# One written-out order of 1169 steps replaced by another in a fused attention and mixing kernel

## The chip, the cores and the metric

The kernel runs on one core of a Trainium2 chip. The metric is device time in microseconds (us), the median of the runs shown. The engines are called as in the profile: PE (TensorE, matrix products) with PEld (its weight loads), DVE (VectorE), ACT (ScalarE), POOL (GpSimd) and SP (SyncE, which here issues the DMAs).

## The reference

```python
# q, k, v, f_logit: (4, 8, 768, 48)
f = 1 / (1 + exp(-f_logit))
for t in range(S):                                  # gated linear attention
    state = f[:, :, t, :, None] * state + einsum('bhd,bhe->bhde', k[:, :, t], v[:, :, t])
    y[:, :, t] = einsum('bhd,bhde->bhe', q[:, :, t], state)
x = y.transpose(0, 2, 1, 3).reshape(4, 768, 384)
theta = x @ w_theta                                 # mixing, w_theta (384, 384)
zr, zi = x * cos(theta), x * sin(theta)
u = x + einsum('ts,bsd->btd', w_tok_r, zr) + einsum('ts,bsd->btd', w_tok_i, zi)
return u + maximum(u @ w_ch, 0)
```

The weights come as 64-bit floats and are turned into 32-bit ones on the chip.

## The kernel before

The sequence of each of the four batches is cut into six chunks of 128 tokens, so that there are 24 chunks, m = 0 to 23. The tile framework runs with a manual schedule: the tuple ORDER names every step in turn, the n-th occurrence of a name being its n-th instance, and each engine gets its instructions in the order in which the steps stand there. Semaphore waits follow from the data and from the buffers. A suffix moves a step from its usual engine: /P to POOL, /D to DVE, /A to ACT. A suffix does nothing for a step whose function names its engine outright (d2 and ro). PLACES says which buffer of its kind each tile gets: "b" are the four single PSUM banks, "a" the two wide PSUM tiles, "z" the rotated values and the raw weights, "wp" the weights, "ut" the three buffers of the result.

The steps of a chunk in attention:

- lf, lk, lq, lv load the gate, key, query and value (SP).
- gc clamps the gate (DVE, or POOL, line 269), go opens it with an exponential and a logarithm (ACT, lines 274 and 275), gs is the running sum (DVE, line 279), ge takes two exponentials (ACT, lines 286 and 287), gp keeps the chunk's end (POOL), gq and gk multiply query and key (lines 294 and 299).
- ke transposes the key (PE, line 347), kt copies it out of PSUM, up builds the state sums (PE, line 362), sa and st add them up, sm fades the state. sc makes the scores (PE, line 333), ma masks them (DVE, line 339). qs and ou make the output (PE, lines 393 and 401), xc copies it, xt transposes it (PE, line 411), xs copies that into the result tile.

The steps of the mixing:

- lw loads a part of the weights; d1, d2, d3 decode it (DVE line 215, ACT line 220, DVE lines 225 and 226), di scales it, d4 and d5 split it in a high and a low half (lines 176 and 250; e4 and e5 do so for w_ch).
- th makes the angles (PE, line 442); for m from 6 on it takes the split forms that xh and xl make. tn, se, ab bring the angle into range, tr takes sine and cosine (ACT, lines 465 and 466) and ro multiplies them with x (DVE, line 475). zh and zl split the product.
- f0, f1, f2 are the token products, 48 of each (PE, line 498); for the first batch (n below 12) in full 32 bits, four profiled matmuls each, after that six matmuls in the faster form. v adds the sum to the result tile, uh and ul split it, c is a channel product (PE, line 516), cv finishes (DVE, line 530), so stores (SP, line 534).

tr and the pair go and ge need different ACT function tables, and each change from one to the other loads a table (lines 259 and 465). Line 176 is a helper that copies for many steps.

Of the kernel before, what the change touches and what calls it, by code (L numbers as in the profile page):

```python
# [17 lines left out]
B, H, S, D = 4, 8, 768, 48  # L18
DM = H * D
P = 128  # L20
# [32 lines left out]


PLACES = {
    "a": "0110110101001010110101010101010101010101010101010",
    "b": ("012301230120123023300300002121123222230230203120310202001031023333312312023011203100000023"
        "1030303030032123123211120303031"),
    "f": "012012012012012012012012",
    "k": "012012012012012012012012",  # L60
    "q": "012012012012012012012012",
# [3 lines left out]
    "ut": "01201201",  # L65
    "v": "012012012012012012012012",
    "w": "010101010101010101010101",
    "wp": "0123456789abcdefghijklmno013245687cd",
    "x": "012012012012012012012012",
    "z": "0123450123412342342350421350421350421",  # L70
}
ORDER = (
# [36 lines left out]
)  # L109


# [627 lines left out]
```

## Time and profile before

| | us |
|---|---|
| median of three runs | 337.82 |
| lowest and highest run | 337.38, 338.60 |
| time of the profiled execution | 338.16 |
| span of its instructions | 335.5 |

The profiled execution took 338.16 us, 2.66 us more than the span of its instructions. PE is busy for 316.8 us of the span; matmul ends are modelled, and short waits between matmuls can hide in that number.

### The profile page before, as it was taken

How to read it: one execution, taken by the hardware profiler on the slowest of the kernel's cores; microseconds unless marked ns; L12 is line 12 of the kernel's file. 1: busy time of each engine (PE TensorE's matmuls, PEld its weight loads, DVE VectorE, ACT ScalarE, POOL GpSimd, SP SyncE). 2: the span in 40 equal slices, each digit the busy share in tenths (PEclk: the TensorE clock that was granted, in tenths of full speed). 3: DMA queues.
4: the chain of work that ended last, by engine and by line, in shares of the span. 5: the costliest groups of instructions: out<-in, count | busy, mean ns of one | idle time of the engine just before them, and what ended most of it. 6: DMA issues, size and time to landing. Idle time of an engine off the chain costs nothing.

```text
span 335.5 us, 9996 instructions
## 1 busy us (share of the span) xinstructions
PE 316.8 (94%) x4320; PEld 280.7 (84%) x4320; DVE 243.4 (73%) x394; ACT 192.9 (58%) x321; POOL 112.3 (33%) x109
## 2 busy tenths in 40 slices
PE   0798999999999999999999999999999999999993
PEld 0685676567676789999999999999999999999992
DVE  5999999999999899968659777774526677441031
ACT  6789977787696799847468253953805342310010
POOL 2452074318100146265371248143800521103110
PEclk9999999999999999999999999999999999999998
DMA  7989779758660463240405353250122102000022
GB/s 266 395 244 304 254 249 340 249 181 308 243 212 17 150 225 111 91 156 15 130 3 168 115 160 117 88 178 0 33 73 79 49 2 73 0 2 0 0 73 77
DMA packets 21619, 45.54 MB, mean 136 GB/s; under 512 B 2369, under 2 KB 5441, under 8 KB 21569
## 3 DMA queue, kind: packets, MB, share of 16 engines
q1 hardware_dynamic: 21568, 44.84, 39.6%
q8 instruction: 36, 0.59, 0.7%
q14 instruction: 15, 0.11, 0.1%
HBM read 40.11 MB, written 4.72 MB: 134 GB/s over the span
## 4 chain that ended last, share of the span: by engine, by line
PE 83%; DVE 9%; ACT 2%; DMA 2%; issue 2%; DVEq 0%; ACTq 0%
PE pm L498 47%; PE pch L516 10%; PE pth L442 9%; PE wide L401 4%; PE wide L393 3%; PE wide L333 3%; PE pxt L411 2%; PE psk L347 2%; PE wide L362 2%; DVE f L279 2%; DMA out_dram<-ut 1%; DVE z L475 1%; DVE raw L215 1%; DMA f<-in_f_dram 1%; DVE k L299 1%
## 5 line engine op out<-in xcount | busy, mean ns | idle before, releaser
L498 PE MATMUL pm<-wp,z 128*128 128x384 f32 x648 | 117.1, 336 | 0.0
L498 PEld LDWEIGHTS pm<-wp,z 128*128 128x128 f32 x648 | 112.4, 188 | 0.0
L498 PE MATMUL pm<-value,z 128*128 128x384 f32 x144 | 49.3, 487 | 0.2 <-DVE z L475 0.2
L516 PE MATMUL pch<-uhl,wch 128*128 128x384 f32 x216 | 40.2, 339 | 0.4 <-DVE ut L176 0.4
L498 PEld LDWEIGHTS pm<-value,z 128*128 128x128 f32 x144 | 26.3, 190 | 15.9 <-DVE value L226 0.5
L516 PEld LDWEIGHTS pch<-uhl,wch 128*128 128x128 f32 x216 | 37.5, 188 | 1.0 <-DVE ut L176 0.7
L290 POOL COPY pes<-p 128x4 f32<-128x4 f32 x24 | 11.4, 476 | 72.6 <-ACT p L286 68.2
L502 DVE TENSOR_TENSOR ut<-pm,ut 128x384 f32<-128x384 f32 x24 | 13.1, 552 | 29.8 <-PE pm L498 29.8
L176 ACT CAST uhl<-ut 128x384 fp32r<-128x384 f32 x18 | 9.2, 509 | 41.5 <-DVE ut L502 41.5
L279 DVE TENSOR_TENSOR_SCAN f<-carry,f 128x512 f32<-128x512 f32 x24 | 29.1, 1222 | 0.7 <-ACT f L275 0.7
L433 POOL TENSOR_TENSOR xl<-ut,xh 128x384 fp32r<-128x384 f32 x13 | 13.5, 1041 | 46.1 <-DVE xh L176 29.1
L286 ACT ACTIVATE p<-f 128x512 f32<-128x512 f32 x24 | 15.1, 628 | 21.7 <-DVE f L279 21.3
L509 POOL TENSOR_TENSOR uhl<-ut,uhl 128x384 fp32r<-128x384 f32 x13 | 13.5, 1047 | 37.0 <-DVE uhl L176 18.6
L347 PE MATMUL psk<-ident,k 128*128 128x128 f32 (+1 forms) x96 | 16.8, 302 | 8.9 <-DVE k L299 8.8
L269 POOL TENSOR_SCALAR f<-f 128x512 f32<-128x512 f32 x14 | 23.3, 1668 | 1.5 <-DMA f<-in_f_dram 1.5
L530 DVE SCALAR_TENSOR_TENSOR ut<-pch,ut 128x384 f32<-128x384 f32 x24 | 13.0, 553 | 14.7 <-PE pch L516 14.4
L482 POOL TENSOR_TENSOR z<-w,z 128x768 fp32r<-128x768 f32 x9 | 17.4, 1931 | 17.8 <-ACT z L176 9.6
L442 PE MATMUL pth<-wth,xh 128*128 128x384 f32 x108 | 23.0, 348 | 0.0
L299 DVE SCALAR_TENSOR_TENSOR k<-f,k 128x512 f32<-128x512 f32 x24 | 19.5, 813 | 3.7 <-ACT f L287 3.6
L401 PEld LDWEIGHTS wide<-v,sc 64*64 64x64 f32 x768 | 15.0, 140 | 8.1 <-issue 4.7
L347 PEld LDWEIGHTS psk<-ident,k 128*128 128x128 f32 (+1 forms) x96 | 11.9, 148 | 11.6 <-POOL pes L290 8.8
L475 DVE TENSOR_TENSOR w<-w,x 128x768 f32<-128x768 f32 x18 | 18.1, 1010 | 4.0 <-ACT w L466 4.0
(84 smaller groups left out, 607.3 us busy)
## 6 DMA issues: line engine op xcount, KB each, us to landing
v<-in_v_dram SPq DMA_DIRECT2D x24, 384.0 KB, 4.4
f<-in_f_dram SPq DMA_DIRECT2D x24, 256.0 KB, 3.6
k<-in_k_dram SPq DMA_DIRECT2D x24, 256.0 KB, 4.1
q<-in_q_dram SPq DMA_DIRECT2D x24, 256.0 KB, 3.9
raw<-in_w_r_dram SPq DMA_DIRECT2D x12, 384.0 KB, 5.1
raw<-in_w_i_dram SPq DMA_DIRECT2D x12, 384.0 KB, 5.6
out_dram<-ut SPq DMA_DIRECT2D x21, 192.0 KB, 2.4
raw<-in_w_theta_dram SPq DMA_DIRECT2D x3, 384.0 KB, 5.5
```

What stands on the lines that cost most here:

```text
L269: on(nc.vector).tensor_scalar(ft, ft, F_MIN, None, op0=ALU.max)
L279: nc.vector.tensor_tensor_scan(fl, carry[:, pairs(h)].rearrange("p n t -> p (n t)"), fl, 0.0, ALU.mult, ALU.add)
L286: nc.scalar.activation(ps_[m][:, pairs(h)], ft, AF.Exp, scale=-1.0)
L299: nc.vector.scalar_tensor_tensor(kt, loaded["f", m][:, pairs(h)], E_TOP, kt, op0=ALU.min, op1=ALU.mult)
L347: nc.tensor.transpose(psks[m][:used(m), p, :], loaded["k", m][:, p, :used(m)], ident)
L401: nc.tensor.matmul(out[HALF[t], j, p, :], scs[m][HALF[a], j, p, :], v2[HALF[a], t, p, :], start=(t == 0 and m % NC == 0 and p == 0), stop= ...
L433: on(nc.vector).tensor_tensor(xls[m], src, xhs[m], op=ALU.subtract)
L442: nc.tensor.matmul(pths[m], l, r, start=(n == 0), stop=(n == len(ms) - 1))
L475: nc.vector.tensor_tensor(zs[m] if full else w, w, xs[m].unsqueeze(1).to_broadcast([P, 2, DM]), op=ALU.mult)
L482: on(nc.vector).tensor_tensor(zs[m][:, 0], ws[m], zs[m][:, 1], op=ALU.subtract)
L498: nc.tensor.matmul(pms[g, d], l, r, start=(s == 0 and i == 0), stop=(s == NC - 1 and i == len(ms) - 1))
L516: nc.tensor.matmul(pcs[g, d], l, r, start=(es[0] == 0 and n == 0), stop=(es[-1] == KD - 1 and n == len(ms) - 1))
```

## The change

The same 1169 steps stand in another order, and the tables of buffers follow it. No function changes, and each name occurs as often as before. The suffixes differ for some steps. DVE's steps by suffix: tn/D 8 for 6, xs/D 9 for 6, uh/D 12 for 6, xh/D as before, one di/D, d4/D 3 for 4, zh/D 6 for 9, kt/D and xc/D 4 for 5. POOL's: gq/P 11 for 9, xl/P 13 for 11, zl/P 13 for 9, sm/P 10 for 11, ul/P 10 for 13. ACT's: ab/A 17 for 14. The diff has all rows of the first third that the prediction speaks of, a stretch of the later part and the end.

```diff
--- before
+++ after
 PLACES = {
-    "a": "0110110101001010110101010101010101010101010101010",
-    "b": ("012301230120123023300300002121123222230230203120310202001031023333312312023011203100000023"
-        "1030303030032123123211120303031"),
+    "a": "0110110011001011001010101010110101010101010101010",
+    "b": ("012301230231202030020222223102131331001201230210212012022020313113103032031201301232321230"
+        "2320320202103213231213012210321"),
...
-    "wp": "0123456789abcdefghijklmno013245687cd",
-    "z": "0123450123412342342350421350421350421",
+    "wp": "0123456789abcdefghijklmno01245679deh",
+    "z": "0123450123412341341350412350412350412",
 }
 ORDER = (
-    "lf gc go lf gc go lf gs lk lq gc gs ge gk gq ke go gp lv sc ge gp gs lk lw lq kt lv lf gk d1 lk lw gq/P lf",
-    "up lq sa d2/P ke kt st ge d3 di d4 qs lv up ma gp ou xc lw sm/P sa gk ke st d1 lf d2 gq gc/P go sm/P d5 gs",
-    "qs gc/P d1 kt lk sc up go sa ma st ge gp gk lq lk d3 lv xt xs lf ou xc gq gs di d2/P gc/P ke kt lq xt go d3",
-    "gs th lw gc ge gp tn se lv gq qs gk sc up ma lq d1 xs go gs sm/P ab/A th ge gq ke kt lk gp ou sa st sm xc xt",
-    "gk d2 xs qs d3 sc up lw ge tr ma tn ro se lv ab gp lq ke kt th tn se sa st ou xc f1 xt xs/D lk qs gk sc tr",
-    "up ma sm/P lf lf d1 ab/A tr ro ro/P ke kt/D gc/P gc/P go sa lv th f0 go gs ou xc gq/P sc up lf gs ma qs sa",
-    "st ge lk gk xt gp f0 d4 f1 tn se xs th lq d2/P lw ke kt d3 sm lk gq/P ou xc/D tn ge se lv d1 sc up ma qs",
-    "d2/P xt f1 f2 f2 xs sa lw gc/P d1 ab ab/A d2 d3 d3 lw d1 f2 lw go gs d5/P th tr ro st tn sm/P gp lv lq gk d1",
-    "gq lq se tr d2 lk f0 ab/A f0 f1 ou ke ro f0 lf tr xc qs d3 kt sc up lw lw d1 xt ro/P f0 d2 d3 d2/P xs f1 f1",
-    "f1 d3 gc/P f1 d1 v lq ge d2 lv go lf xh gp gk gq/P sa st v ke ma xl/P ou sc kt up sm/P gs ge xc/D qs xt sa",
-    "st d4 gc/P xs d4/D f2 d4 ma lk gq lw d1 d2 lf gc/P th tn f2 f2 d3 lw d1 go lq gk ke d3 f1 go gs gs f1 uh kt",
...
-    "sc up xc ma gq qs ke kt/D sa f2 f2 ul uh ul/P f1 f0 ro/P v uh lv ul v c c xh/D cv cv lq c cv zh lf ou xc/D",
-    "sc up v ma gp ge sa qs xl/P uh/D uh gp ul ul gc/P go xt gq xt zl/P lk gk th tn se st ab tr lv sm/P c c so so",
-    "so lf xs/D cv gc/P lk c xh/D xl th zl/P xs xh xl/P ro/P ke kt ou xc/D cv sc up qs xt tn zh/D f0 lv se ab/A",
-    "cv xs th sa st f1 f1 zl/P f1 lq lq go ma so so xh tn/D se ab/A f2 f2 f2 so gs ge gp gs gk tr ro/P tr sm ke",
...
-    "se ab/A zh/D zl tr ro f2 f2 zh zl f0 so f1 f0 f1 f1 f1 f0 v uh/D f1 f2 f1 f1 f1 f2 v f2 so v uh/D uh ul/P f0",
-    "f2 f2 f0 f0 f0 f0 f0 v f2 ul/P ul/P c c cv cv so f1 c cv v so so uh uh f2 f2 v ul/P c ul/P uh ul c c rv cv",
-    "cv cv",
+    "lf gc go gs ge lf lf gc gc/P gp lk gk lq lq lk lk gq go gs go gs ge gp lv ke kt sc lf gq lq up gc gk ke sa",
+    "st ge gq/P qs go gp lv kt up gk sm/P ke gs ge lw d1 d2/P ma ou lw d1 xc lf lk sa st d2/P lv lf lq sc gc/P kt",
+    "qs lw d3 di lk d4 lv lq gk gc/P up ma sm/P go d3 di/D xt sa xs ou xc go lw gs ke gp gq st gs d1 ge gk gq lf",
+    "lf lv th sm qs sc kt up ma tn lq gp lw xt xs/D sa ke d2 st ou se th lk ge ab gp sm/P kt tr xc/D xt xs d3 ro",
+    "tn sc qs up gc/P gc/P th sa ma ou lk go go xc se gs f1 gk lv tn/D ke st gq/P gs ab/A xt xs/D d1 lq qs ge lv",
+    "kt sc up tr d2 se th ma sm/P sa ro/P gk ab/A gp tr d4/D d1 lk d4/D lq sc ou ke kt ro/P lw f0 xc xt xs d3 qs",
+    "up sa tn se d1 lv gq/P ge gq/P ma th st f0 qs tn/D lk d2/P ab/A tr gk se ou ke f2 f2 kt d5 xc d2/P d3 sm d3",
+    "ro/P lf lf lw xt lw d1 sc up lq xs th ma lw gc/P go gs f1 f1 f1 lv ou ab/A sa d2 lf gp d1 st d2/P gc/P d3 d3",
+    "lw go qs tn f2 f2 ge gk se gs tr ro d1 f0 gc/P xc ke ab/A gp sm tr ro kt/D f0 d2/P go f2 sc lv up xt xs d3",
+    "d5 f0 lk gq ge f2 f0 d4 f1 lw d1 d4 d4 gs lq gq/P d4 sa f1 v d2/P gk ke kt ma ou xc lq st uh/D xh/D lw v uh",
+    "v uh d1 xl/P d3 d2/P d1 sc up qs gp lk lf gc d4 xt th tn go sm/P sa st d3 ge lk se gk f0 lf f1 f1 xs xh xl/P",
+    "ul/P gs ke d2/P f0 kt gp gc/P ma ou xc gq lv lw sc up d4/D qs xt xs ge lw ma gp d1 sm sa f0 th d2/P d3 lf gk",
...
+    "tr ke kt lk gk tn/D se ou lv sc up ma xc qs lf gp d5/P gq/P ab/A ul/P ul xt ke sm sa st f1 lq kt gs ge gp tr",
+    "xs/D f0 c ro/P cv lk gc/P go v gk c cv f2 c so f1 sm/P gc go ke uh/D gs gq/P ou xc sc up qs f2 ul/P f1 zh/D",
+    "zl/P cv f2 so so lk xh xl th ge gp sa kt v uh lq f2 ro/P f2 zh xt tn/D se ma ab/A xs/D lv f2 gk gq/P xh xl/P",
+    "ou sc up xc gs v qs sa st xt ge ke sm th lv ul/P uh/D ul c zl lk tr ro xs tn xh/D ma cv c kt se ou xc sc up",
+    "ab qs lf tr xl/P lq gk ke kt/D ro zh cv xt xs zl th tn/D ma f2 f2 so lk f0 f2 lf lf c zh zl/P xh/D f0 se",
+    "ab/A sa st lq tr ro/P zh/D xl/P th ou xc tn lv sc up cv so gc/P qs xt gc se ab/A f1 f1 f1 f0 tr ro ma f1 zh",
+    "zl/P zl f0 sm sa st so gq/P gp sm go gs ge f0 f0 f2 gp xs/D xh/D xl f2 f2 gk ke v gq uh f1 go gs ge gp kt f1",
...
+    "cv f2 f2 f1 f2 f1 f0 f1 zh/D zl/P f0 se ab tr ro/P so zh f2 zl/P f2 f0 f2 f2 so f1 v uh f1 f1 f1 f1 v v f2",
+    "f1 f1 f1 uh f0 uh/D f0 f0 f0 f0 f2 ul ul f2 f2 f2 fl so f1 f0 v uh/D ul/P ul v v c c c cv cv c uh/D uh cv ul",
+    "ul c c rv so cv cv cv so so",
 )
```

## Rows read from the trace of the kernel before

**Rows 1.** The page: span, and busy us, share and instructions of each engine.
```profile
span 335.5 us, 9996 instructions
...
PE 316.8 (94%) x4320; PEld 280.7 (84%) x4320; DVE 243.4 (73%) x394; ACT 192.9 (58%) x321; POOL 112.3 (33%) x109
```

**Rows 2.** Windows over five stretches: busy us of each engine (instructions), clock, DMA.
```profile
0.00:39.30 39.30, 27.00 (x580) 20.86 (x580) 34.38 (x55) 31.90 (x55) 12.74 (x23) 1.00 0.86 294
39.30:86.80 47.50, 47.38 (x714) 32.23 (x715) 46.29 (x71) 37.42 (x63) 21.74 (x18) 1.00 0.73 250
86.80:190.00 103.20, 103.20 (x1439) 91.88 (x1439) 87.88 (x138) 71.47 (x118) 36.37 (x31) 1.00 0.40 133
190.00:329.80 139.80, 139.19 (x1591) 135.78 (x1590) 74.36 (x132) 52.11 (x89) 41.42 (x37) 1.00 0.17 56
329.80:335.50 5.70, 0.00 (x0) 0.00 (x0) 0.53 (x2) 0.00 (x0) 0.00 (x0) 0.76 0.32 112
```

**Rows 3.** Waits of PE: who for whom, total us, times, longest.
```profile
PE psk L347 <- DVE k L299: 8.8, 1, 8.8
```

**Rows 4.** Timeline of the start: start us, duration us, engine, line, operation.
```profile
5.29 0.61 ACT L274 ACTIVATE f<-f 128x512 f32<-128x512 f32 x1
5.41 1.23 DVE L279 TENSOR_TENSOR_SCAN f<-carry,f 128x512 f32<-128x512 f32 x1 [0.71 <-ACT f L275]
...
6.67 0.63 ACT L286 ACTIVATE p<-f 128x512 f32<-128x512 f32 x1
6.87 1.22 DVE L279 TENSOR_TENSOR_SCAN f<-carry,f 128x512 f32<-128x512 f32 x1
...
8.01 0.69 DVE L299 SCALAR_TENSOR_TENSOR k<-f,k 128x512 f32<-128x512 f32 x1
...
9.21 1.22 DVE L279 TENSOR_TENSOR_SCAN f<-carry,f 128x512 f32<-128x512 f32 x1
...
11.29 1.27 POOL L294 TENSOR_TENSOR q<-q,p 128x512 f32<-128x512 f32 x1 [0.88 <-DMA q<-in_q_dram]
11.32 1.66 DVE L215 TENSOR_SCALAR raw<-raw 128x768 int32<-128x768 int32 x1
```

**Rows 5.** Timeline at the key transposition of chunk 10.
```profile
85.97 0.69 DVE L299 SCALAR_TENSOR_TENSOR k<-f,k 128x512 f32<-128x512 f32 x1
...
86.82 0.60 PE L347 MATMUL psk<-ident,k 128*128 128x128 f32 x4
```

**Rows 6.** Lines by form, whole kernel: busy us, mean ns, idle before and releasers.
```profile
L339 DVE TENSOR_TENSOR sc<-wide,causal 128x512 f32<-128x512 f32 x24 | 16.4, 682 | 4.6 <-PE wide L362 2.7 <-ACT w L458 1.7
...
L259 ACT ACT_TABLE_LOAD x11 | 14.1, 1283 | 1.0 <-PEq L729 0.8
...
L225 DVE SCALAR_TENSOR_TENSOR raw<-raw 128x768 int32<-128x768 int32 x14 | 13.3, 952 | 0.0
...
L453 DVE SCALAR_TENSOR_TENSOR w<-w,pth 128x384 f32<-128x384 f32 x24 | 13.2, 548 | 10.5 <-ACT w L447 10.3
...
L294 DVE TENSOR_TENSOR q<-q,p 128x512 f32<-128x512 f32 x15 | 12.9, 861 | 0.0
...
L215 DVE TENSOR_SCALAR raw<-raw 128x768 int32<-128x768 int32 x14 | 9.6, 686 | 0.0
...
L250 DVE TENSOR_TENSOR wp<-value,wp 128x768 fp32r<-128x768 f32 x6 | 5.7, 948 | 0.0
...
L176 DVE CAST uhl<-ut 128x384 fp32r<-128x384 f32 x6 | 2.1, 353 | 0.0
```

**Rows 7.** Chain of the work that ended last: start us, us, what.
```profile
81.56 1.29 PE pm L498 x4
...
196.08 3.67 DMA out_dram<-ut
...
201.57 1.84 PE pch L516 x9
```

**Rows 8.** The stores of results (line 534): from issue to landing.
```profile
DMA to landing us min/median/max: 1.9/2.4/5.3
```

32 rows, old and new, of the table ORDER are left out of this document.

## The prediction

> **What bounds the kernel now.** I read the page first: PE is busy for 316.8 of 335.5 us [rows 1], so at most 18.7 us can be won or added to while its work stays the same, and the change leaves PE's instructions alone. The windows tell where those 18.7 us lie [rows 2]: 39.3 - 27.0 = 12.3 us before 39.3 us, 0.1 us from there to 86.8, nothing to 190, 0.6 us from there to 329.8, and 5.7 us after PE's last matmul. So the start and the end are the only large holes. In the start DVE is the engine that is full: 34.4 of 39.3 us, so 4.9 us idle, and in the next stretch 46.3 of 47.5 us, so 1.2 us idle [rows 2]. The waits of PE say the same: the longest is the one for the first gated key, 8.8 us [rows 3]. From 39 us on PE has no holes, but DVE stays only just ahead of it. The timeline at chunk 10 shows this: DVE's key product starts at 85.97 and lasts 0.69, so ends at 86.66, and PE's transposition of that key starts at 86.82 [rows 5]. After 86.8 us DVE falls to 87.9 of 103.2 us and then to 74.4 of 139.8 [rows 2], and the pressure is off.
>
> My reading is therefore: PE's total is fixed, and what an order can change is how late PE is made by DVE up to about 87 us, plus small holes later. The place to compare the two orders is the transposition ke n=10, where before has 0.16 us to spare between producer and consumer and the clock of the whole rest hangs on it.
>
> **The change, part by part.** No step is added or removed, so PE's sum stays. The granted clock is full in every stretch up to the end of PE's work [rows 2], and I count PE's steps at the same price in both orders.
>
> *DVE's work ahead of ke n=10.* I count the steps that stand in ORDER up to gk n=10 and run on DVE: 109 before, 114 after. Per kind the difference is: more by one each se, v, xh, xs, d4, and by two tn, all of them 128-row passes near 0.55 us, for which the row of se stands (0.548 us); 7 x 0.55 = 3.85. More by one uh at 0.35 and one d5 at 0.95. More by one sm and one di, which I put at 0.5 each between the rows at 0.35 and 0.55 [rows 6]; di on DVE has no row of its own. Together 3.85 + 0.35 + 0.95 + 1.0 = 6.15 us. Fewer by two gq at 0.86, one d1 at 0.69, one ma at 0.68, one xc at 0.55, and one ab at 0.5, between the same bounds: 4.14 us [rows 6]. So DVE has 2.0 us more to do before that key is ready.
>
> *PE's work ahead of ke n=10.* The same PE steps stand ahead of it in both orders but for one more token product of the first batch, four profiled matmuls or 1.29 us [rows 7]. A PE that has 1.3 us more to do meanwhile loses 2.0 - 1.3 = 0.7 us, not 2.0.
>
> *The first 10 us.* Before, ACT opens the second chunk's gate (go n=1, from 5.29 us) while DVE sums the first (gs n=0, 5.41 to 6.64), and DVE goes on with gs n=1 at 6.87 while ACT takes the exponentials of ge n=0, from 6.67; only then comes gk n=0, at 8.01 [rows 4]. In the new order ge n=0 stands ahead of go n=1 on ACT, and gc n=1 behind gs n=0 on DVE. gk n=0 is no earlier, since ge n=0 waits for the same sum; DVE has only gc n=1 (some 0.4 us) to fill the 1.4 us up to 8.01, and gs n=1 comes behind gk, gq and go n=1, at about 9.3 us, where before had gs n=2 (9.21). One gs of 1.22 us has moved out of a gap that was free, against one gc that moved into it from another gap. ACT, which waits 1.3 us for that first sum with go n=1 queued behind, hands the lateness on to gs n=2 and gs n=3. I take 1.1 us more idle on DVE; the bounds are 0.7 (the scan's 1.22 less the clamp's share) and 1.5 (with a further 0.4 at gs n=3).
>
> *What is given back.* Between 39.3 and 86.8 us DVE is idle for 1.2 us [rows 2], the short waits of an engine that runs ahead. A DVE that is later meets fewer of them. Bounds 0 and 1.2; I take half, -0.6.
>
> *The order between 10 and 39 us.* At the first token product (f1 n=0) DVE has 42 steps ahead of it instead of 46. A sum (1.22), a key (0.69), a query (0.86), a mask (0.68), a d1, a d5 and a d3 of two instructions near 0.95 are moved behind it, four steps of about 0.55 ahead of it [rows 4, 6]. So the product can start roughly 4 us sooner, and PE's holes before 39 us shrink. But the moved steps are needed by ke n=10, and PE runs into DVE again there, so the early start is not worth 4 us; it is in the sum above already.
>
> *A store that a copy waits for.* In the last 140 us the chain shows a transfer to the output of 3.67 us (from 196.08), and then PE's channel product at 201.57 [rows 7]. The result tile is one of three buffers: xs n=15 writes a buffer whose old result is being stored. Before has the three stores and then xs n=15 with no PE step between. The new order has th n=14, token products and xt between, some 4 us of PE, against a landing of 2.4 us in the median and 5.3 at most [rows 8]. Most of the 0.6 us of PE idle in that stretch [rows 2] should go: -0.6, bounds 0 and -0.6.
>
> *What lies beside other work.* The new order changes ACT's table 12 times each way (counted: go or ge behind a tr) instead of 11, two loads more in all at 1.28 us [rows 6], and four more up to tr n=6. ACT has 47.5 - 37.4 = 10.1 us of air in that stretch [rows 2], so I put this at nothing; without that cover it would cost 4 x 1.28 = 5.1 us. POOL is busy for a third of the span [rows 1], so the steps handed to it cost nothing on its own queue. The loads stand in another order on SP; DMA engines are at 0.86 and 0.73 in the first two stretches [rows 2], and the first weights are asked for after more of the small loads and also used later, so nothing here too. The end is the same: three channel products, three finishing passes and one store.
>
> The sum: +0.7 (ke n=10) +1.1 (start) -0.6 (idle absorbed) -0.6 (store) = +0.6 us. On the profiled execution, 338.16 us, that is 338.8; the median of the runs is 0.34 us under that execution, so I forecast 338.4 us. A measurement of this kernel can tell about 0.3%, or 1.0 us, from no change, so this counts as no change.
>
> **The rivals.**
>
> *Nothing is absorbed (slower).* DVE stays the limit from the start to ke n=10, each of its short waits recurs, and the later hole appears at another copy: xs n=18 in the new order has some 3 us of PE work between its last store and itself, near the landing's median. Then +0.7 + 1.1 (to 1.5) + 0 + 0 to 0.3: +1.8 to 2.5, about 340.0 us. For it speaks that DVE is 97% full from 39.3 to 86.8 us (46.3 of 47.5); against it, that the 1.2 us of idle time show DVE running ahead of its suppliers now and then [rows 2]. It decides as soon as gk n=10 ends more than 1.6 us later than 86.7.
>
> *POOL holds DVE up more often (slower).* At 11.29 POOL starts a query product of 1.27 us; DVE's d1, which starts at 11.32, takes 1.66 us against a mean of 0.686 over its kind [rows 4, 6]. So such a meeting costs about 1 us. [...] Ahead of ke n=10 both orders have 21 long POOL steps, but the meetings fall otherwise, and I cannot read from the order which. Two more of them than before: +0.6 + 2 x 1.0 = +2.6, 340.4 us.
>
> *DVE is freed (faster).* With two such meetings fewer, all of the 1.2 us absorbed and the store's wait gone: 0.7 + 1.1 - 1.2 - 0.6 - 2.0 = -2.0, 335.8 us. For it speaks the early start of f1 n=0; against it, the count at ke n=10. It decides if gk n=10 ends before 85.6 us.
>
> **How the numbers follow.** No measurable change, around 338.4: 0.43. Nothing absorbed: 0.22, meetings on POOL: 0.15, so slower 0.37. DVE freed: 0.20. The range runs from the faster rival, 335.8, raised a little because all three of its terms must come together, 336.1, up to the second rival with 0.5 us of the start's upper bound, 340.9. The likeliest case's own range is 336.8 to 338.8.
>
> **What the profile after would show.** PE's products of the first batch start near 35 us instead of 39.3. The window up to the transposition of chunk 10 has PE idle of about 13 us or a little more, and that transposition starts near 88.5 to 89.5 us (it has 1.3 us more PE work ahead). DVE's gs n=1 starts near 9.3 us. No output transfer stands in the chain near 175 to 200 us. The forecast is wrong if gk n=10 is no longer the step that PE meets last, if ACT's waits show up ahead of PE's, or if new holes of PE appear after 90 us.

## The result and the profile after

The changed kernel takes 340.13 us at the median of four runs (338.64 to 340.82), the kernel before 337.67 in its four runs beside them (337.38 to 338.60). The ratio is 1.0068, with a 95% interval of 1.0047 to 1.0090: slower by 0.7%, or 2.3 us. That is inside the predicted range, but the case forecast as likeliest was no change.

The profiled execution of the changed kernel took 338.64 us, its fastest run, and that of the kernel before 338.16, above its median. These two profiles are thus only 0.5 us apart where the medians differ by 2.5, so that a good part of the loss at the median is not in this pair; twelve more executions with a profile follow below.

The page, with the span and the engines, answers to [rows 1]:

```profile
span 336.9 us, 10023 instructions
...
PE 316.7 (94%) x4320; PEld 279.5 (83%) x4320; DVE 245.6 (73%) x397; ACT 196.4 (58%) x320; POOL 122.9 (36%) x109
```

PE has the same 4320 products and the same busy time. The span is 1.4 us longer, but the execution only 0.5: the time outside the span fell from 2.66 to 1.74 us. The windows over the same five stretches answer to [rows 2]; the second now ends at 87.0 and the last starts at 330.1, as the same steps end there:

```profile
0.00:39.30 39.30, 26.83 (x584) 20.33 (x585) 32.42 (x56) 31.75 (x53) 17.26 (x25) 1.00 0.86 304
39.30:87.00 47.70, 47.70 (x716) 31.94 (x713) 46.53 (x75) 43.17 (x69) 15.65 (x13) 1.00 0.73 247
87.00:190.00 103.00, 102.13 (x1428) 90.56 (x1428) 88.97 (x134) 74.55 (x119) 54.05 (x42) 1.00 0.39 125
190.00:330.10 140.10, 140.04 (x1598) 136.69 (x1596) 77.15 (x134) 46.94 (x82) 35.98 (x29) 1.00 0.18 59
330.10:336.90 6.80, 0.00 (x0) 0.00 (x0) 0.53 (x2) 0.00 (x0) 0.00 (x0) 0.69 0.27 94
```

Up to 87 us PE's holes are the same 12.5 us (39.30 - 26.83, and none). Two stretches are worse: 0.87 us of hole is new between 87 and 190, and the tail is 6.8 instead of 5.7 us. One is better: the 0.6 us between 190 and the end are gone.

The timeline at chunk 10 answers to [rows 5]. DVE's key ends at 86.99 and PE takes it at 87.05, so that DVE is still only just ahead of PE. PE has no hole there, as the 47.70 of 47.70 us above show:

```profile
86.31 0.68 DVE L299 SCALAR_TENSOR_TENSOR k<-f,k 128x512 f32<-128x512 f32 x1
...
87.05 0.44 PE L347 MATMUL psk<-ident,k 128*128 128x128 f32 x2
```

The timeline of the start answers to [rows 4]; the running sum of the second chunk starts at 9.30, as forecast (the first token product starts at 37.40, against 39.30 before and the 35 of the forecast):

```profile
6.65 0.77 DVE L269 TENSOR_SCALAR f<-f 128x512 f32<-128x512 f32 x1
...
8.09 0.69 DVE L299 SCALAR_TENSOR_TENSOR k<-f,k 128x512 f32<-128x512 f32 x1 [0.67 <-ACT f L287]
...
9.30 1.22 DVE L279 TENSOR_TENSOR_SCAN f<-carry,f 128x512 f32<-128x512 f32 x1
```

The waits of PE answer to [rows 3]. The second row is new:

```profile
PE psk L347 <- DVE k L299: 8.9, 1, 8.9
...
PE pch L516 <- DVE ut L530: 0.9, 1, 0.9
```

This is a new hole of PE after 90 us, which the prediction's last paragraph names as a sign of being wrong. The timeline around that wait shows what is late. POOL splits z (zl) from 131.05 to 132.89. DVE's split d5 n=4, started 0.27 us later, lasts 2.38 us, where [rows 6] has a mean of 0.948 for its form. cv n=3 (line 530) stands behind it on DVE, and PE's channel product waits for cv:

```profile
131.05 1.84 POOL L482 TENSOR_TENSOR z<-w,z 128x768 fp32r<-128x768 f32 x1
...
131.32 2.38 DVE L250 TENSOR_TENSOR wp<-value,wp 128x768 fp32r<-128x768 f32 x1
...
133.63 0.55 DVE L530 SCALAR_TENSOR_TENSOR ut<-pch,ut 128x384 f32<-128x384 f32 x1
...
134.23 0.62 PE L516 MATMUL pch<-uhl,wch 128*128 128x384 f32 x2 [0.87 <-DVE ut L530]
```

The chain around 200 us answers to [rows 7]: no transfer to the output is in it any more.

```profile
199.55 1.60 PE pth L442 x9
201.14 3.12 PE pch L516 x18
```

The end needs a view that the prediction did not read: the instructions at the end of the program (line 735, the engines' last semaphores and drains), with count, durations and the starts of the first and the last one. First the kernel before, then after:

```profile
L735 PEldq DRAIN  x2: 8/40/73, 333.5 to 335.0; - x2
...
L735 DVEq EVENT_SEMAPHORE  x2: 21/21/21, 334.9 to 335.4; - x2
L735 PEldq EVENT_SEMAPHORE  x2: 51/51/51, 334.9 to 335.4; - x2
```

```profile
L735 PEldq DRAIN  x2: 8/40/73, 333.6 to 336.7; - x2
...
L735 DVEq EVENT_SEMAPHORE  x2: 21/21/21, 335.0 to 336.9; - x2
L735 PEldq EVENT_SEMAPHORE  x2: 51/51/51, 336.5 to 336.9; - x2
```

Before, PE and DVE pass their first semaphore together at 334.9. After, DVE passes it at 335.0 and PE at 336.5, though PE's first drain was as early as before (333.6 against 333.5). PE has nothing left to compute there, and all others wait for it.

### The profile page after: what moved, and what is told of

Read it like the earlier page. It is cut to its first block, busy times and chain, and to the rows that moved or that the text cites. A ratio compares the mean times of both kernels' runs of the same rounds, so it can differ in the third digit from the quotient of the medians.

```text
span 336.9 us, 10023 instructions
## 1 busy us (share of the span) xinstructions
PE 316.7 (94%) x4320; PEld 279.5 (83%) x4320; DVE 245.6 (73%) x397; ACT 196.4 (58%) x320; POOL 122.9 (36%) x109
## 4 chain that ended last, share of the span: by engine, by line
PE 88%; DVE 5%; DMA 3%; issue 1%; ACT 1%; SPq 0%; DVEq 0%
PE pm L498 48%; PE pch L516 11%; PE pth L442 11%; PE wide L401 4%; PE wide L333 3%; PE wide L393 3%; PE psk L347 3%; PE pxt L411 3%; PE wide L362 2%; DMA raw<-in_w_theta_dram 2%; DVE f L279 1%; DMA f<-in_f_dram 1%; DVE sc L339 1%; DVE k L299 0%; DVE ut L530 0%
## 5 line engine op out<-in xcount | busy, mean ns | idle before, releaser
L482 POOL TENSOR_TENSOR z<-w,z 128x768 fp32r<-128x768 f32 x13 | 24.2, 1859 | 36.0 <-ACT z L176 21.2
L279 DVE TENSOR_TENSOR_SCAN f<-carry,f 128x512 f32<-128x512 f32 x24 | 30.8, 1287 | 5.9 <-ACT f L275 5.8
L294 POOL TENSOR_TENSOR q<-q,p 128x512 f32<-128x512 f32 x11 | 16.4, 1491 | 28.4 <-ACT p L286 26.0
L176 ACT CAST uhl<-ut 128x384 fp32r<-128x384 f32 x12 | 6.0, 510 | 33.6 <-PE pch L516 21.1
L274 ACT ACTIVATE f<-f 128x512 f32<-128x512 f32 x24 | 15.0, 626 | 9.1 <-POOL f L269 5.7
```

The source lines that it names most:

```text
L279: nc.vector.tensor_tensor_scan(fl, carry[:, pairs(h)].rearrange("p n t -> p (n t)"), fl, 0.0, ALU.mult, ALU.add)
L294: on(nc.vector).tensor_tensor(qt, qt, ps_[m][:, pairs(h)], op=ALU.mult)
L482: on(nc.vector).tensor_tensor(zs[m][:, 0], ws[m], zs[m][:, 1], op=ALU.subtract)
```

## The experiments

Each kernel ran with the kernel before on the same chip; that one's median was 337.50 us (13 runs) beside the first four kernels below, then 337.64 (26 runs) beside the next four, 337.85 (29) beside the three after those and 337.66 (17) beside the last. One theory stood against another: the new order makes PE late by DVE at the start (the prediction's terms), or the loss lies in places that the prediction put at nothing, the meeting of POOL and DVE at 131 us and the end.

**The new order once more**, nothing changed.

> The new order once more, unchanged, beside the others on one chip. In its first profile PE's last matmul ends only 0.3 us later than before (330.0 against 329.7 us) while its other runs lie up to 2.2 us above that run. Theory A (the loss lies in waits of DVE behind POOL that fall otherwise from run to run): median 339.5 to 340.5 us, and this profile shows long DVE passes at other places and PE holes in other sums. Rival B (the loss is a fixed one in the order and in the end of the program): the profile repeats the first one within 0.3 us at PE's last matmul.

Measured: 339.69 us (6 runs), ratio 1.0066 (1.0046 to 1.0085). The profile has the long split again, 2.39 us at 131.23, and PE late at the end again. So both belong to the order, not to one execution.

**The new order with the old first steps.**

```diff
-    "lf gc go gs ge lf lf gc gc/P gp lk gk lq lq lk lk gq go gs go gs ge gp lv ke kt ...
+    "lf gc go lf gc go lf gs gc/P ge gs gp lk gk lq lq lk lk gq go gs ge gp lv ke kt ...
```

> The new order with the first steps of the old one: the second clamp and the second opening ahead of the first sum and the first exponentials, the second sum ahead of the first key product. Theory A (the start makes DVE later by 1.1 us, and DVE sets PE's holes up to the key transposition of chunk 10): that transposition comes 0.7 to 1.1 us earlier than in the new order (87.05 us in its first profile) and the median falls by as much. Rival B (after the start DVE waits for loads, ACT or PE anyway): within 0.3 us of the new order.

Measured: 340.06 us (5 runs), ratio 1.0082 (1.0062 to 1.0101): nothing gained. ke n=10 starts at 86.69 instead of 87.05. DVE waits for two transfers between 8 and 40 us; the first profile of the new order had only the second of these waits, with 0.7 us, and the repeat neither:

```profile
DVE f L269 <- DMA f<-in_f_dram: 1.0, 1, 1.0
DVE raw L215 <- DMA raw<-in_w_theta_dram: 0.6, 1, 0.6
```

**The old order with the new first steps.**

```diff
-    "lf gc go lf gc go lf gs lk lq gc gs ge gk gq ke go gp lv sc ge gp gs lk lw ...
+    "lf gc go gs ge lf lf gc lk lq gk gq go gs gc ke go gp lv sc ge gp gs lk lw ...
```

> The old order with the first steps of the new one, the reverse of the start experiment. Theory A: PE's transposition of chunk 10 (86.8 us before) comes 0.7 to 1.1 us later, and the median rises by as much, since DVE has 0.16 us to spare there. Rival B: no change within 0.3 us.

Measured: 340.70 us (6 runs), ratio 1.0099 (1.0077 to 1.0122), that is 3.2 us more, and ke n=10 at 89.39 instead of 86.82:

```profile
89.39 0.60 PE L347 MATMUL psk<-ident,k 128*128 128x128 f32 x4
```

Among PE's waits one for ACT has grown, from 0.2 us to 2.8, for the copy of a transposed key (kt):

```profile
PE wide L362 <- ACT ktok L176: 2.8, 1, 2.8
```

So the first steps do cost what the prediction argued, and more, but in the old order, and by a wait for ACT that it did not price. In the new one, taking them back gives nothing.

**The meeting: d5 n=4 moved behind cv n=3.**

```diff
-    ... sm sa st th tn/D se d5 ge lv xs c cv xh ab/A tr ...
+    ... sm sa st th tn/D se ge lv xs c cv d5 xh ab/A tr ...
```

> The new order with one DVE step, the split d5 of number 4, moved behind the finishing pass cv of number 3. In the first profile it starts at 131.3 us while POOL splits z, takes 2.38 us instead of 0.95, and PE waits 0.9 us at 134.2 for cv behind it. Theory A (this meeting is a hole that the whole rest inherits): the hole goes and the median falls by 0.8 to 1.1 us against the new order. Rival B (another wait of DVE takes its place, or the spread of the runs is larger than this hole): less than 0.4 us.

Measured: 338.98 us (8 runs), ratio 1.0038 (1.0024 to 1.0053), 0.7 us under the new order on the same chip. The timeline shows that the meeting is not gone, d5 still meets POOL's pass and takes 1.71 us; but cv now stands ahead of it, and PE's wait for cv is no longer in the list:

```profile
132.37 1.85 POOL L482 TENSOR_TENSOR z<-w,z 128x768 fp32r<-128x768 f32 x1
...
132.85 0.56 DVE L530 SCALAR_TENSOR_TENSOR ut<-pch,ut 128x384 f32<-128x384 f32 x1
...
133.33 1.71 DVE L250 TENSOR_TENSOR wp<-value,wp 128x768 fp32r<-128x768 f32 x1
```

Both lengths of d5 follow from POOL's pass: from d5's start to POOL's end it is 1.57 us in the first profile and 0.89 here, and d5 ends 0.81 and 0.82 us after that. In the windows the stretch from 130 to 140 us has no hole of PE, where the repeated new order had 0.88 us (PE busy 9.12 of 10). First the repeat, then this kernel:

```profile
130.00:140.00 10.00, 9.12 (x111) 8.43 (x110) 9.57 (x14) 5.79 (x10) 5.91 (x4) 1.00 0.30 93
```

```profile
130.00:140.00 10.00, 10.00 (x116) 9.64 (x115) 9.66 (x16) 5.69 (x11) 5.95 (x4) 1.00 0.43 130
```

This profile also has a start 1.4 us later than the first two of the new order. DVE's timeline names a transfer: gc n=3 got its gates 5.0 us after their load was issued (at 8.99), in the first profile after 3.4 us at most (8.81 to 12.18, without a wait).

```profile
13.95 0.43 DVE L269 TENSOR_SCALAR f<-f 128x512 f32<-128x512 f32 x1 [1.50 <-DMA f<-in_f_dram]
```

**The waits for transfers at the start.** One kernel puts gc n=3 on POOL, the other asks for lw n=0 ahead of those gates.

```diff
-    ... lv ke kt sc lf gq lq up gc gk ke sa
+    ... lv ke kt sc lf gq lq up gc/P gk ke sa
```

```diff
-    ... lv ke kt sc lf gq lq up gc gk ke sa
-    ... sm/P ke gs ge lw d1 d2/P ...
+    ... lv ke kt sc lw lf gq lq up gc gk ke sa
+    ... sm/P ke gs ge d1 d2/P ...
```

> The new order with one step changed: gc n=3, which reads the fourth chunk of gates, goes to POOL (as in the order before) and leaves DVE. In the profiles of the new order this step stands on DVE right behind gq n=1 and ahead of gk n=1 and sa n=0, and its load is issued at 8.8 to 9.0 us and lands 3.3 us later in two profiles (no wait) and 5.0 us later in the third (DVE waits 1.50 us, and every PE step from ke n=1 to the end is 1.4 us later). Theory A (a DVE step that waits for a transfer makes the new order's start vary, and the median run has such a wait): DVE has no wait for that transfer, PE's work missing by 40 us is 19.5 us or less, and the median falls by 0.7 to 1.2 us, to 338.5 to 339.0. Rival B (the late landing was that one run's, and other things make the spread): the profile looks like the other two of the new order, 19.5 to 20 us missing by 40, and the median stays within 0.3 of 339.7. Rival C (POOL takes 1.5 to 1.9 us for the step where DVE takes 0.42, go n=3 and gs n=3 come later): PE's missing work grows by 0.5 or more by 40 us, the median is 340 or more.

> The new order with the first weight load step (lw n=0) moved ahead of the load of the fourth chunk's gates on SP, so that its transfers are issued at about 5 us, as in the order before, and not at 10.1 us behind three other loads. In the first profile of the new order d1 n=0 waits 0.74 us on DVE for this transfer, which lands at 16.74. Theory A (the order of the loads is what makes the start slower, the prediction's step that put it at nothing is wrong): d1 n=0 has no wait, the gates' load that gc n=3 waits for lands at 12.2 or earlier since less stands beside it, PE's work missing by 40 us falls by 0.5 us or more, and the median by 0.5 to 1.0, to 338.7 to 339.2. Rival B (nothing here, as predicted: DVE's work ahead absorbs 0.7 us at that place): within 0.3 of 339.7. Rival C (the weights take the bandwidth of the first chunks): sc n=0 and up n=0 start later than 9.9 and 12.4 us by 0.5 or more, the median is 340.2 or more.

Measured: 340.01 us (8 runs), ratio 1.0057 (1.0037 to 1.0077), and 339.80 us (7 runs), 1.0061 (1.0038 to 1.0084). Neither differs from the new order. In the first DVE waits 0.7 us for the weights and no more for the gates; in the second 1.2 us for the gates and no more for the weights. Theory A fell for each alone; what the two kernels leave untested stands with the last experiment.

**Code that never runs: the new order with four more products.** Behind the last step stands a branch to a slow path for rare inputs. That path is not taken for these inputs, and PE jumps over it. Four matmuls more in that path change nothing that runs, only where PE's last instructions stand in its program.

```diff
                     nc.tensor.matmul(bc, sel.rearrange("p j m -> p (j m)"), vr[:, hs], start=True, stop=True)
+                    if p + e + h == 0:
+                        for _ in range(4):
+                            nc.tensor.matmul(bc, sel.rearrange("p j m -> p (j m)"), vr[:, hs], start=True, stop=True)
```

> The new order with four more matmuls in the branch that is not taken (the recurrence for the rare case), so that nothing that runs changes, but PE's instructions behind the branch stand further on in its program. In the four profiles of the new order PE's sequencer has 50 instructions against 47 before, and its first semaphore of the end barrier comes 1.5 to 1.9 us behind those of ACT and DVE; with 47 it comes within 0.1 us. [...] Rival B (PE is late there because of something in the new order that ran, and not because of the place of its instructions): the semaphore is 1.5 us late still, the median within 0.3 of 339.7. Rival C (the barrier is mended in the span, but what lies outside the span takes all of it back): span 1.5 shorter, median unchanged.

Measured: 338.28 us (12 runs), ratio 1.0011 (0.9996 to 1.0026). PE is on time at the end, as its own and DVE's rows show:

```profile
L738 PEldq DRAIN  x2: 8/40/73, 335.5 to 337.1; - x2
...
L738 DVEq EVENT_SEMAPHORE  x2: 21/21/21, 336.9 to 337.4; - x2
L738 PEldq EVENT_SEMAPHORE  x2: 51/51/51, 336.9 to 337.4; - x2
```

By the ratios this takes back 1.0066 - 1.0011 = 0.55%, or 1.9 us, of the 2.3. The median falls by 1.4 us, from 339.69 (the repeat, on another chip) to 338.28, and so does the median span, from 338.0 to 336.6. The time outside it did not grow: it stays at 1.70, so nothing of the gain is lost there.

**The old order, moved by two instructions.** One more transposition in the path not taken.

```diff
+                if m == 0:
+                    nc.tensor.transpose(px[:, :P], u_slice(m)[:, 0, :], ident)
```

> The old order with one more transposition in the branch that is not taken (a weight load and a matmul, two PE instructions), nothing that runs is changed. Theory A (place of PE's last instructions in its program; with three more they are late by 1.5 to 1.9 us): one of PE's last four instructions comes 1.5 us or more behind the other engines', the span is 1.5 us longer, 336.3 instead of 334.8 at the median, the median time 0.5 to 0.9 longer, 338.0 to 338.4. [...] Rival B (something that ran): no change, 337.5.

Measured: 337.86 us (12 runs), ratio 1.0004 (0.9989 to 1.0020). The instruction that is late is now PE's second drain, 1.8 us after a first semaphore that was on time:

```profile
L737 PEldq DRAIN  x2: 8/40/73, 332.6 to 336.0; - x2
...
L737 PEldq EVENT_SEMAPHORE  x2: 51/51/51, 334.1 to 336.1; - x2
```

PE's sequencer has 47 records in the old order and 50 in the new one. With two instructions more than the old order has, the gap falls behind the first semaphore; with three more, one instruction ahead of it. Counted in these instructions both are the same place of the program, and the instructions move past it. That excludes a cause in the work that ran. What takes the 1.5 and 1.8 us at this place, no row shows. The span grew by 1.3 us at the median (336.2 against 334.9), and the time outside fell from 2.70 to 1.70, so the time hardly moved, where theory A had it 0.5 to 0.9 us longer.

**The old order with the same four products.**

> The old order with the same four matmuls more in the branch that is not taken (16 PE instructions by the pairs of weight load and matmul that such a product shows in the trace). So far, time outside the span and end of PE: old order 2.7 us outside at the median of 26 runs, PE on time at the end; old order with two PE instructions more 1.70 outside, PE late by 1.8 us at its last drain; new order 1.7 outside, PE late by 1.5 to 1.9 at the semaphore ahead of it; new order with sixteen more 1.70 outside, PE on time. [...]

Measured: 337.19 us (12 runs), ratio 0.9981 (0.9961 to 1.0001). PE is on time and the time outside the span is 1.74 us instead of 2.63. The median is 0.66 us under that of the old order, and the interval still just holds 1.

**Both mends in the new order**: the four products, and d5 n=4 behind cv n=3; then the old first steps as well.

> The new order with the four matmuls in the branch that is not taken, and d5 n=4 moved from ahead of cv n=3 to behind it. Theory A (the two effects are separate and add): 0.7 to 1.0 below the 338.28 of the first alone, 337.3 to 337.6; PE's missing work is the same at 130 and at 140 us (0.1 to 0.2 more, not 1.3). Rival B (the meeting is only moved, DVE's long pass comes where it costs the same): 338.3.

> As the run before, and with the old order's first steps (go n=1 and n=2 ahead of ge n=0, gs n=1 ahead of gk n=0 and gq n=0). The prediction put the start of the new order at +1.1 us; alone it gave 0.3 us of PE's missing work and nothing in the median, while the new order's first steps in the old order cost 3.2 us. Theory A (in the new order DVE and the loads, not ACT, set the first 20 us, so the first steps' order is worth nothing): within 0.4 of the run before, 337.2 to 337.8. Rival B (the start's 1.1 us is there, hidden so far by the spread of the runs): 0.8 to 1.1 less than the run before, 336.3 to 336.6.

Measured: 337.42 us (12 runs), ratio 0.9995 (0.9979 to 1.0011), and 337.38 us (12 runs), 0.9993 (0.9978 to 1.0009). The two mends add: 1.0011 to 0.9995 is 0.5 us by the ratios, and the medians fall by 0.9 (338.28 to 337.42). The first steps give nothing in the new order, for the second time.

**Both changes to the loads together**, in the kernel with both mends: gc n=3 on POOL and lw n=0 early.

> The new order with the four matmuls in the branch that is not taken and d5 n=4 behind cv n=3, as in an earlier run (337.42), and with both steps at the start that wait for transfers changed at once: gc n=3 on POOL and lw n=0 asked for ahead of the fourth gates. In ten profiles with the new order's later part DVE waits 0 to 1.8 us for these two transfers between 8 and 40 us, and ke n=10 starts anywhere from 86.7 to 88.6 us; in three profiles of the old order it waits for none and ke n=10 starts at 86.5 to 86.8. Theory A (these waits are what spreads the start and what is left of the new order's loss; each change alone only moved the wait to the other transfer): no wait of DVE for a transfer in that stretch, ke n=10 near 86.5, median 336.6 to 337.0. Rival B (the start has other sources of delay of the same size, as the two changes alone gave nothing): median 337.2 to 337.7, within 0.3 of the earlier run. Rival C (POOL's longer clamp delays go n=3): 338 or more.

Measured: 337.95 us (12 runs), ratio 1.0004 (0.9983 to 1.0025). No transfer holds DVE itself between 8 and 40 us, but the fourth running sum now waits for ACT's gate go n=3. ACT waits for the clamp gc n=3, which now runs on POOL, and POOL waits for the gates:

```profile
13.41 1.49 POOL L269 TENSOR_SCALAR f<-f 128x512 f32<-128x512 f32 x1 [1.89 <-DMA f<-in_f_dram]
```

```profile
16.25 1.55 DVE L279 TENSOR_TENSOR_SCAN f<-carry,f 128x512 f32<-128x512 f32 x1 [1.44 <-ACT f L275]
```

So the late transfer is not taken away, it is handed on through POOL and ACT. ke n=10 starts at 88.44, and the median lies between the ranges of rival B (up to 337.7) and rival C (338 or more). Theory A is not met, but this kernel did not test what it says.

The chain of the work that ended last shows more than the waits. Between 4 and 40 us it passes through a load in nine of the ten profiles with the new order's later part, and in none of the four with the old one's. In the first profile it is a load of weights, in the new order with four more products a load of values (v), which none of these kernels moved:

```profile
10.61 6.13 DMA raw<-in_w_theta_dram
```

```profile
14.58 7.41 DMA v<-in_v_dram
```

Where the chain passes through the weights or through no load, ke n=10 starts at 86.69 to 87.05 us (four profiles); where it passes through gates or values, at 87.62 to 88.58 (six profiles, this kernel's among them).

## Why the prediction was in range and its likeliest case was not what happened

In ratios to the kernel before, the loss comes apart like this (0.01% is 0.03 us):

| kernel | ratio | us against before |
|---|---|---|
| new order (two measurements) | 1.0068, 1.0066 | +2.3, +2.2 |
| PE's last instructions moved | 1.0011 | +0.4 |
| and d5 n=4 behind cv n=3 | 0.9995 | -0.2 |
| old order, PE's last instructions moved | 0.9981 | -0.6 |

So 1.9 us by the ratios (1.4 by the medians) are the place of PE's code at the end, about 0.5 (0.7 to 1.0 when taken alone) one meeting of POOL and DVE, and with both mended the new order is no slower than the kernel before. The old order gains 0.6 us by the same four products, so the place of the code makes 1.9 - 0.6 = 1.3 us of the difference between the two orders, and the work that runs the other 1.0 (1.0011 against 0.9981), about half of it the meeting. Each of these ratios is known to 0.15 to 0.2%, so these shares are known to some 0.5 us each. With both mended the new order is 0.14% or 0.5 us slower than the old order with its code moved too, inside the intervals of both.

That the time lies in the range is in good part luck: its largest piece, the place of the code, is in none of the prediction's terms.

**"The end is the same."** This is the step that failed. It compared the work of the end, three channel products, three finishing passes and a store, and that part was right: the last store is issued 0.3 us later than before. What follows the store was priced at nothing and cost the new order 1.4 to 1.9 us. The order carries three more semaphore instructions on PE, and these move PE's end in the program.

**POOL's steps "at nothing", and the second rival.** The rival had the meeting of POOL and DVE and nearly the time (340.4), but the wrong place. It looked ahead of ke n=10 and found nothing to tell the orders apart; the meeting that costs stands at 131 us, where DVE is 86% full (88.97 of 103.0) and the prediction held the pressure to be off. An average over 100 us says nothing on a pass that stands right ahead of one for which PE waits; from 130 to 140 us DVE is busy for 9.57 of 10 us. The cost of the meeting is in the trace: d5 takes 2.38 us beside POOL's 1.84 us pass, against a mean of 0.948. (Of POOL's suffixes, xl/P stands 11 times for 13, not 13 for 11 as given with the change.)

**+0.7 from the count of DVE's work, +1.1 from the start.** Neither is borne out in the new order: taking its first steps back gave nothing, twice, and DVE's work ahead of the key did not grow. ke n=10 was to start at 88.5 to 89.5 us; it started at 87.05. In the five profiles whose first steps are the new order's own (and unmended) it lies between 86.88 and 88.57, in three of the old order between 86.50 and 86.82. The count of steps was right, 125 DVE instructions up to the key before and 130 after, but the busy time fell instead of rising by 2.0 us. The windows from 0 to the end of gk n=10 show it, before and after:

```profile
0.00:86.70 86.70, 74.28 (x1293) 53.05 (x1293) 80.57 (x125) 69.23 (x117) 34.49 (x41) 1.00 0.79 270
```

```profile
0.00:86.99 86.99, 74.52 (x1297) 52.28 (x1297) 78.94 (x130) 74.91 (x121) 32.91 (x38) 1.00 0.79 273
```

DVE is at 78.94 us, 1.6 less, with five instructions more. The extra d5 is of half size and took 0.55 us, and the extra d4, di and sm 0.35 to 0.36 each, where 0.95, 0.55 and twice 0.5 were put. Prices from the means of the whole kernel also hid that the same pass costs different amounts in the two orders. The decode d1 shows it (lines by form, up to 86.9 us): before, with the 1.66 us pass beside POOL in [rows 4], and after.

```profile
L215 DVE TENSOR_SCALAR raw<-raw 128x768 int32<-128x768 int32 x12 | 8.5, 708 | 0.0
```

```profile
L215 DVE TENSOR_SCALAR raw<-raw 128x768 int32<-128x768 int32 x11 | 6.2, 566 | 0.7 <-DMA raw<-in_w_theta_dram 0.7
```

A single d1 less saved 2.3 us and not 0.69. Part of that is one execution's: in the old order moved by two instructions the same twelve passes take 7.3 us.

```profile
L215 DVE TENSOR_SCALAR raw<-raw 128x768 int32<-128x768 int32 x12 | 7.3, 607 | 0.0
```

This was the third rival's term, fewer meetings of POOL and DVE ahead of chunk 10, and it happened. Of the 21 long POOL steps that the prediction counted ahead of ke n=10 in both orders, two stand behind gk n=10 in the new one. What it gave went into idle time of DVE (6.1 to 8.1 us), above all in the first 39 us (4.9 to 6.9).

**-0.6 for the store.** The wait went away as forecast. But the two later profiles of the old order (with code moved) have PE without a hole there too: the chain goes through PE alone from 194 to 206 us. The term was the size of one execution's late transfer, not of the order.

**The loads "nothing here too".** This step failed too, though no run prices it. DVE waits for transfers in the new order, up to 1.8 us in a profile, and in no profile of the old one, and the chain passes through a load at the start of nine of ten profiles. The three kernels that changed the loads were no faster, but each left a late load in the chain, so they do not rule the loads out. What makes ke n=10 vary by 1.7 us in the new order, against 0.3 in three profiles of the old one, goes together with the load in the chain; no run tested it. The times of the old order's runs spread as widely (336.26 to 339.02 on one chip), so three profiles are few to call its start steady.

**The first rival**, nothing absorbed at 340.0 us, hit the time almost exactly. The sign it named is absent from the first profile: gk n=10 was to end 1.6 us later than before and ended 0.3 us later. But that profile is of the fastest run. In three executions that were the slowest of their kernels' runs, or the slowest but one, ke n=10 starts at 88.39 to 88.58 us, so a late start may well be part of the median. What the runs exclude is the largest of its terms, the 1.1 us from the order of the first steps.

What is left open as well: why the old order spends 2.7 us outside the span where it spends 1.74 with its code moved by sixteen instructions. A gap like the one of 1.5 to 1.9 us, just behind PE's last instruction, would do that; this is a guess, and nothing in the trace shows it. How much of the median the late loads cost is open too.

## What to carry to other kernels

Before a difference below 1% is laid to an order, look at the last two microseconds: if one engine passes the final semaphores later than the others with nothing to compute, move its code, for instance by a few instructions in a path that is not taken, and measure again (here the median fell by 1.4 us). Price a pass by its own row beside what POOL does at that moment, and look for long DVE passes that meet POOL right ahead of a pass that PE waits for, however idle DVE is on average (here 2.38 us against a mean of 0.948, in a stretch where DVE is 86% full). Take a wait seen in one profile as a term only if a second profile of the same kernel has it too. When a step that waits for a load is moved, read the chain again before the loads are ruled out: another engine may wait in its place (here POOL waited 1.89 us for the gates, and DVE 1.44 us for ACT).

## What the hardware showed that was not expected

At the end PE's sequencer stands in a branch instruction (line 657) for 3.49 us in the kernel before and 3.27 in the new order, so this is no difference between them; the other record of that branch takes 0.095 us. Before and after:

```profile
L657 PEldq COMPARE_BRANCH  x2: 95/1794/3493, 327.5 to 329.9; - x2
```

```profile
L657 PEldq COMPARE_BRANCH  x2: 95/1684/3272, 327.6 to 330.2; - x2
```

In four profiles of the new order another 1.5 to 1.9 us pass between two of PE's last four instructions, and 1.8 us in the old order moved by two instructions. With four more products in the path that is not taken, the new order has no such gap: PE and DVE pass their first semaphore together at 336.9.

The profile names nothing that PE waits for, neither in the 3.27 us at the branch nor in the gap behind it. What PE does there is not shown, only that the gap goes with the place of its instructions in the program.
